# Scan units in pairs: the products of one tile shape of two units together

## The chip, the cores and the metric

The kernel runs on one core of a Trainium2 chip. The core has a matrix engine (TensorE, "PE" in the profile, with its weight loads as "PEld"), a vector engine (VectorE, "DVE"), a scalar engine (ScalarE, "ACT"), a general engine (GpSimd, "POOL") and a queue that issues DMA transfers (SyncE, "SP"). Each engine runs its own list of instructions in order, and they wait for each other through semaphores. TensorE writes into PSUM, which has eight banks of 512 float32 columns on 128 partitions. The metric is the time of one execution in microseconds (us), the median of several runs.

## The reference

Two stages. The first is a chunked scan (a state space layer) over 4 batches of 8 heads, 768 steps, head size 32, state size 16; the second is a gated feed-forward layer over the 3072 resulting rows of 256.

```
for each chunk of the sequence:
    M       = (C B^T) * exp(cum_i - cum_j) * causal
    y       = M x + (C state) * exp(cum)
    state   = decay_full * state + sum_j decay_from_j * B_j x_j
x    = y as rows of 256
gate = sigmoid(x @ w_gate);  val = x @ w_val
out  = (gate * val) @ w_out
```

All numbers are float32. The feed-forward matrices are 256 x 1536 (twice) and 1536 x 256.

## The kernel before, in words

The sequence is cut into 6 chunks of 128 steps. A **unit** is one chunk of one batch, with all 8 heads: 24 units, numbered u = 4 x chunk + batch. Behind each chunk, 512 rows go through the feed-forward layer: 12 pairs of a gate product and a value product, then 4 output products (one for each batch). From chunk 1 on these products run on operands that are split in a high and a low part of type fp32r, three passes for a gate or value product of 128 input rows and a 512- and a 256-column pass for an output product. The feed-forward work of chunk k is what TensorE does while the units of chunk k + 1 are computed in between.

A unit of chunk 1 or later has these steps on TensorE, and others around them:

- `products`: B and C are transposed (`pt`, L375 and L376, in a bank of the pool `ps_mm`), and ScalarE copies them to `bct` (L380, L384).
- `multiply`: B by C, four matmuls of 32 rows by 128 columns, one for each quarter of the partitions, which run side by side in the four tiles of that shape. Each writes 256 columns of one of four banks (`pcb`, L397). The pool `ps_cb` has one such tile, so the four banks hold one unit's products, half full.
- `decays`: VectorE's scan makes the matrix of decays (`ab`, L408). `before`: VectorE makes `cd` (L424), C times the decay from the chunk's start.
- `result`: VectorE multiplies `pcb` by the decays into `m` (L430). Then TensorE adds in one bank (`py`, pool `ps_y`, one bank) the part of the state (`py<-cd,sb`, L447, two matmuls of 128 x 128) and the part of the chunk (`py<-m,xn`, L453, eight matmuls of 128 rows by 32 columns, four side by side). In the same step follows the `multiply` of the next unit. So a unit's block on TensorE has three tile shapes: 128 x 128, 128 x 32, 32 x 128. A float32 matmul shows as two passes, the transposes as one.
- ScalarE takes `py` to the high part (L463), VectorE subtracts for the low part (L466) and transposes the rest (L471), from which `state` updates the state (L477) and the matrix `sb` (L485, mostly GpSimd).

Gate and value products (`pg`, `pv`, L699), output products (`po`, L728 for 512 columns and L729 for 256) and the transposes share the three banks of `ps_mm` in turn. A gate product is emptied by ScalarE's sigmoid (L654), a value product by VectorE's multiplication `g<-pv,g` (L669); then ScalarE rounds (L673) and GpSimd subtracts (L675) to make the two parts `h` that the output product needs. An output product is emptied by ScalarE's copy (L733) and VectorE's addition (L735), and its row block is written out (L741).

The order of all engines' instructions is written by a planner when the kernel is built (`run`): each task is a generator of steps with an engine, a cost, what it needs and makes, and a due time. The planner keeps a clock for each engine and picks, among the steps that can begin first, the task that is due first. The constants `UNIT_T`, `UNIT_D`, `AHEAD` and `STATE` set the due times of units, their loads and their state updates against the feed-forward work of the chunk; `FFN1` is where chunk 1's products are due. What the planner knows is costs and due times; the chip runs each engine's list in that order and waits where data is late.

## Time and profile before

| | before |
|---|---|
| median of 3 runs | 390.72 us (390.13 to 391.47) |
| profiled execution: its own time, its span | 389.6 us, 387.8 us |
| TensorE, weight loads busy | 378.4 us (98%), 287.4 us (74%) |
| VectorE, ScalarE, GpSimd busy | 197.0 us, 151.1 us, 159.7 us |
| output products of chunk 0, then chunk 1's gate products begin | 72.3 us, 102.4 us |
| gate products of chunks 2, 3, 4, 5 begin | 162.2, 220.7, 279.0, 334.2 us |

A row of the timeline has the start in the span, the time that the group takes, the engine, the line of the program, the operation, the tiles written and read, the shape, and the count of instructions merged. The ends of matmuls are modelled and overlap the next start, so TensorE's pace is read from start to start. A remark in brackets tells how long the engine had been idle and what it waited for.

### The profile page before, as it was taken

The page shows a single profiled execution, that of the slowest core. Times are in us where ns is not written, and L with a number is a line of the kernel's source. Part 1 is how long each engine was busy: PE and PEld are TensorE (multiplying, and loading weights), DVE is VectorE, ACT ScalarE, POOL GpSimd, SP SyncE. Part 2 cuts the span into 40 slices and gives each one's busy share as a digit, 9 for nine tenths or more (in the row PEclk, how much of TensorE's full clock was granted, in tenths as well). Part 3 has the DMA queues.
Part 4 walks back from the last instruction along what each step waited for, and adds up shares of the span by engine and source line. Part 5 has one row for each costly group of instructions (what it writes and reads, how often), then busy time and mean ns, then how long its engine had stood idle before and what let it go on. Part 6 is the DMA issues. An engine that isn't in the chain of part 4 may idle for free.

```text
span 387.8 us, 6198 instructions
## 1 busy us (share of the span) xinstructions
PE 378.4 (98%) x2368; PEld 287.4 (74%) x2368; DVE 197.0 (51%) x310; ACT 151.1 (39%) x319; POOL 159.7 (41%) x136
## 2 busy tenths in 40 slices
PE   8789999999999999999999999999999999999995
PEld 4444444677788778878788878788878788888884
DVE  3776878977746477856454356452323320122200
ACT  2564655434456521244441243440243430244400
POOL 2353354475899941035460054460033340045410
PEclk9758999999999999999999999999999999999999
DMA  7999782083700297333314513312100000000000
GB/s 86 236 368 385 100 217 77 5 165 103 124 13 1 24 214 167 56 93 87 45 44 103 94 38 88 40 50 49 47 2 0 2 0 29 27 0 2 0 27 29
DMA packets 107462, 31.39 MB, mean 81 GB/s; under 512 B 76554, under 2 KB 102730, under 8 KB 107434
## 3 DMA queue, kind: packets, MB, share of 16 engines
q1 hardware_dynamic: 107434, 31.01, 34.6%
q8 instruction: 19, 0.31, 0.3%
q14 instruction: 9, 0.07, 0.1%
HBM read 27.66 MB, written 3.34 MB: 80 GB/s over the span
## 4 chain that ended last, share of the span: by engine, by line
PE 92%; SPq 3%; DMA 2%; issue 1%; ACT 0%; POOL 0%; DVE 0%; ACTq 0%
PE pv L699 21%; PE pg L699 21%; PE po L728 15%; PE po L729 7%; PE pg L690 6%; PE po L721 6%; PE pv L690 5%; PE pcb L397 3%; PE py L453 3%; PE py L447 2%; DMA wr<-in_moe_w_val_dram 2%; SPq L267 1%; SPq L253 1%; SPq L293 1%; PE pt L375 1%
## 5 line engine op out<-in xcount | busy, mean ns | idle before, releaser
L675 POOL TENSOR_TENSOR h<-g,h 128x512 fp32r<-128x512 f32 x60 | 87.2, 1454 | 101.0 <-ACT h L673 100.9
L728 PE MATMUL po<-w,h 128*128 128x512 f32 x240 | 86.6, 403 | 0.0
L699 PE MATMUL pg<-xh,w 128*128 128x512 f32 x240 | 85.0, 395 | 0.0
L699 PE MATMUL pv<-xh,w 128*128 128x512 f32 x240 | 84.6, 393 | 0.0
L669 DVE TENSOR_TENSOR g<-pv,g 128x512 f32<-128x512 f32 x60 | 41.3, 688 | 83.7 <-PE pv L699 74.0
L673 ACT CAST h<-g 128x512 fp32r<-128x512 f32 x60 | 37.3, 621 | 80.3 <-DVE g L669 80.3
L729 PE MATMUL po<-w,h 128*128 128x256 f32 x240 | 67.4, 281 | 0.0
L728 PEld LDWEIGHTS po<-w,h 128*128 128x128 f32 x240 | 45.1, 188 | 12.9 <-issue 2.0
L699 PEld LDWEIGHTS pv<-xh,w 128*128 128x128 f32 x240 | 45.0, 188 | 11.4 <-issue 1.7
L654 ACT ACTIVATE g<-pg 128x512 f32<-128x512 f32 x72 | 43.0, 598 | 25.0 <-PE pg L690 15.2
L699 PEld LDWEIGHTS pg<-xh,w 128*128 128x128 f32 x240 | 45.0, 188 | 9.7 <-issue 0.3
L408 DVE TENSOR_TENSOR_SCAN ab<-ab,delta 128x1024 f32<-128x1024 f32 x20 | 47.5, 2378 | 4.1 <-DMA ab<-a_z 4.1
L699 PE MATMUL pg<-xl,w 128*128 128x512 f32 x120 | 46.8, 390 | 0.0
L699 PE MATMUL pv<-xl,w 128*128 128x512 f32 x120 | 46.7, 389 | 0.0
L729 PEld LDWEIGHTS po<-w,h 128*128 128x128 f32 x240 | 45.3, 189 | 0.2
L485 POOL TENSOR_TENSOR sb<-st,of_h 128x256 f32<-128x256 f32 x20 | 20.5, 1027 | 59.5 <-DVE st L477 48.3
L430 DVE TENSOR_TENSOR m<-pcb,ab 128x1024 f32<-128x1024 f32 x20 | 24.4, 1220 | 25.4 <-PE pcb L397 25.3
L323 POOL TENSOR_TENSOR wr<-wr 128x512 int32<-128x512 int32 x18 | 21.8, 1216 | 33.9 <-ACT wr L321 29.7
L733 ACT COPY o<-po 128x256 f32<-128x256 f32 x20 | 7.4, 372 | 62.5 <-PE po L729 60.7
L735 DVE TENSOR_TENSOR o<-po,o 128x256 f32<-128x256 f32 x20 | 8.5, 423 | 43.4 <-ACT o L733 43.2
L699 PEld LDWEIGHTS pv<-xl,w 128*128 128x128 f32 x120 | 22.5, 188 | 4.5
L699 PEld LDWEIGHTS pg<-xl,w 128*128 128x128 f32 x120 | 22.6, 188 | 4.3
(92 smaller groups left out, 428.1 us busy)
## 6 DMA issues: line engine op xcount, KB each, us to landing
ab<-a_z SPq DMA_DIRECT2D x20, 512.0 KB
wr<-in_moe_w_gate_dram SPq DMA_DIRECT2D x6, 512.0 KB
wr<-in_moe_w_val_dram SPq DMA_DIRECT2D x6, 512.0 KB
wr<-in_moe_w_out_dram SPq DMA_DIRECT2D x6, 512.0 KB
out_dram<-o SPq DMA_DIRECT2D x24, 128.0 KB
xn<-in_x_dram SPq DMA_DIRECT2D x10, 256.0 KB
bn<-in_B_dram SPq DMA_DIRECT2D x40, 32.0 KB
cn<-in_C_dram SPq DMA_DIRECT2D x40, 32.0 KB
```

Of the source, the lines that this page charges most:

```text
L323: nc.gpsimd.tensor_tensor(out=lw.bitcast(I32), in0=hw.bitcast(I32), in1=lw.bitcast(I32), op=ALU.add)
L408: nc.vector.tensor_tensor_scan(out=t.rearrange("p h l -> p (h l)"), data0=t.rearrange("p h l -> p (h l)"), data1=delta.rearrange("p h l -> ...
L430: nc.vector.tensor_tensor(out=self.second()[:, :, :L].rearrange("p (q g) l -> p q g l", g=NG), in0=self.pcb[:, :, : NG * L].rearrange("p q ...
L654: nc.scalar.activation(gs[k, f], pm, AF.Sigmoid)
L669: nc.vector.tensor_tensor(out=g, in0=pm, in1=g, op=ALU.mult)
L673: copies[eng](hh, g)
L675: engines[eng].tensor_tensor(out=hl, in0=g, in1=hh.bitcast(F32), op=ALU.subtract)
L690: nc.tensor.matmul(pm, whole[f // 2 * 2 + j][:, kt, fs], xb[0][0][:, kt], start=(kt == 0), stop=(kt == NK - 1))
L699: nc.tensor.matmul(pm, w[:, part, kt, fs], xx[:, kt], start=(i == 0), stop=(i == 3 * NK - 1))
L721: nc.tensor.matmul(acc[:, :DM], hs[k, f][:, js], whole[NF + f // 2][:, f % 2], start=(f == 0), stop=(f == NF - 1))
L728: nc.tensor.matmul(acc, hh, w.rearrange("p i m -> p (i m)"), start=(f == 0), stop=False, skip_group_check=True)
L729: nc.tensor.matmul(acc[:, :DM], hl, w[:, 0, :], start=False, stop=(f == NF - 1), skip_group_check=True)
```

## The change

From chunk 2 on, the two units of a pair of batches (0 and 1, 2 and 3) are one task (`results`). On TensorE first come both units' `py<-cd` matmuls (128 x 128), then both units' `py<-m` matmuls (128 x 32). The first unit's `py` is in `ps_y` as before, the second unit's takes one of the three banks of `ps_mm` until its results are taken; ScalarE and VectorE empty the second unit's first. `multiply` now makes a tile `pcb` of the same four banks for two units: each bank holds 256 columns of the one and 256 of the other. From chunk 2 on it is a task of its own (`multiply_after`, due as early as can be), which waits for the results of the two units before and both transposed copies. Units of chunk 1 stay single; the last of them is followed by the B by C products of the first two units of chunk 2.

Further, the due times change (all units of a chunk are due at one time, their loads 21.9 us ahead of it), steps of units are tied to their predecessor's in order (`bct`, `cd`), three steps of chunk 0 get a planned dependency on the transfers from the tiles that they overwrite (`held`), and the last output product of the last chunk is split: its twelve passes of 512 columns go to its bank, and the twelve low passes of 256 columns to a bank of their own behind them (`po`), with an addition of their own (L811 of the new program).

```diff
-FFN1 = 106.4
-UNIT_T = -15.3
-UNIT_D = 11.6
-AHEAD = 35.0
-STATE = 18.1
+FFN1 = 107.3
+UNIT_T = 3.4
+UNIT_D = 0.0
+AHEAD = 21.9
+STATE = 14.7
...
-            needs = [("bc", u), ("cb", u - 2), ("cd", u - 2)] + ([("x", 0, NB - 1)] if c == 1 else [])
+            needs = [("bc", u), ("bct", u - 1 if c > 1 else -1), ("cb", u - 2), ("cd", u - 2)] + ([("x", 0, NB - 1)] if c == 1 else [])
...
-            then = NB <= u < NB * NCH - 1
-            if then:
-                yield step("pe", 1.9, needs + [("bct", u + 1)], [("y", u), ("cb", u + 1)], cb=1)
-            else:
-                yield step("pe", 1.25, needs, [("y", u)])
+            then = [u + 1] if b < NB - 1 else [u + 1, u + 2]
+            yield step(
+                "pe", 1.25 + 0.65 * len(then), needs + [("bct", v) for v in then], [("y", u)] + [("cb", v) for v in then],
+                cb=1,
+            )
...
-            if then:
-                units[u + 1].multiply()
+            multiply(*(units[v] for v in then))
...
+    def multiply(*two):
+
+        pcb = ps_cb.tile([P, NQ, 2, NG * L], F32, tag="pcb", name=f"pcb{two[0].nm}")
+        for i, u in enumerate(two):
+            u.pcb = pcb[:, :, i]
+            for q in range(NQ):
+                qs = slice(32 * q, 32 * q + 32)
+                nc.tensor.matmul(
+                    pcb[:, q, i], u.bct[qs, 0], u.bct[qs, 2:4].rearrange("p g l -> p (g l)"), start=True, stop=True,
+                )
+
+    def multiply_after(*us):
+
+        then = [u + 2 for u in us]
+        yield step("pe", 1.3, [("y", u) for u in us] + [("bct", u) for u in then], [("cb", u) for u in then], cb=1)
+        multiply(*(units[u] for u in then))
+
+    def results(*two):
...
+        needs = [("lo", us[0] - 2), ("lo", 2 * NB - 1)] + [(k, u) for u in us for k in ("xn", "cd") + ("bdec",) * more] + [("S", u - NB) for u in us]
+        yield step("pe", 2.05, needs, [("y", u) for u in us], banks=1)
+        for t, pool, tag in zip(two, (ps_y, ps_mm), ("py", "mm")):
+            t.py = pool.tile([P, NG, LB], F32, tag=tag, name=f"py{t.nm}")
+
+        for t in two:
+            for g in range(NG):
+                nc.tensor.matmul(
+                    t.py[:, g, :L], sb[t.b][:, g].rearrange("p q d -> p (q d)"), t.cd,
+                    start=(g == 0), stop=False, skip_group_check=True,
+                )
+        for t in two:
+            xn = got["xn", c, t.b // 2][:, t.b % 2]
+            for g in range(NG):
+                for q in range(NQ):
+                    nc.tensor.matmul(
+                        t.py[32 * q : 32 * q + 32, g, : t.w], xn[:, NQ * g + q, :], t.m[:, NG * q + g, : t.w],
+                        start=False, stop=True, skip_group_check=True,
+                    )
+
+        for t, u in zip(two[::-1], us[::-1]):
...
+        last = (k, j) == (NCH - 1, NB - 1)
...
+            if last:
+                nc.tensor.matmul(acc, hh, w.rearrange("p i m -> p (i m)"), start=(f == 0), stop=(f == NF - 1))
+                continue
...
+            low = ps_mm.tile([P, 512], F32, tag="mm", name="po")
+            for f in range(NF):
+                nc.tensor.matmul(
+                    low[:, :DM], hs[k, f][:, 1, js], wo[f // 2][:, f % 2, 0, :], start=(f == 0), stop=(f == NF - 1)
+                )
...
+            if last:
+                yield step("dve", DVE_HALF)
+                nc.vector.tensor_tensor(out=o, in0=low[:, :DM], in1=o, op=ALU.add)
...
-        task(due, f"result{u.nm}", u.result())
+        if c < 2:
+            task(due, f"result{u.nm}", u.result())
+        elif b % 2:
+            if u.u < NB * NCH - 1:
+                task(-300.0, f"then{u.nm}", multiply_after(u.u - 1, u.u))
+            task(due, f"result{u.nm}", results(pair.pop(), u))
+        else:
+            pair.append(u)
```

What it does to the lists of instructions shows at three places. In the names, `pg3_3` is the gate product of chunk 3 and column block 3, `py4_1` the result of chunk 4, batch 1; the last number is the tile's own.

TensorE before, among the gate and value products of chunk 3, at unit 1 of chunk 4:

```order
L699 MATMUL pg3_3_2292<-xh3_1685,w2_733 128x512
L447 MATMUL py4_1_2307<-cd4_1_2188,sb1_115 128x128 x2
L453 MATMUL py4_1_2307<-m4_1_2094,xn4_0_1798 32x144 x8
L397 MATMUL pcb4_2_2318<-bct4_2_2299 128x256 x4
L699 MATMUL pv3_3_2328<-xh3_1685,w3_887 128x512
```

One unit's block: its two result shapes and, behind them, the B by C products of the next unit.

TensorE now, for units 0 and 1 of chunk 4:

```order
L760 MATMUL pv3_3_2274<-xh3_1787,w3_887 128x512
L519 MATMUL py4_0_2287<-cd4_0_2214,sb0_114 128x128 x2
L519 MATMUL py4_1_2288<-cd4_1_2252,sb1_115 128x128 x2
L527 MATMUL py4_0_2287<-m4_0_1966,xn4_0_1790 32x144 x8
L527 MATMUL py4_1_2288<-m4_1_1987,xn4_0_1790 32x144 x8
L375 MATMUL pt4_3_2313<-eye_88,bn4_1_1818 128x128
L376 MATMUL pt4_3_2313<-eye_88,cn4_1_1823 128x128
```

Both units' results stand in one block of two shapes; the transposes of unit 3 follow it in place of B by C products.

TensorE now, a gate product later, where the B by C products of units 2 and 3 stand:

```order
L760 MATMUL pg3_4_2316<-xl3_1788,w4_915 128x512
L760 MATMUL pg3_4_2316<-xh3_1787,w4_915 128x512
L489 MATMUL pcb4_2_2337<-bct4_2_2268 128x256 x4
L489 MATMUL pcb4_2_2337<-bct4_3_2328 128x256 x4
L760 MATMUL pv3_4_2365<-xh3_1787,w5_933 128x512
```

The B by C products of the two units stand together, by themselves, between a gate and a value product.

VectorE before, at the `cd` of unit 3 of chunk 4:

```order
L669 TENSOR_TENSOR g3_7_2428<-pv3_7_2421,g3_7_2428 128x512
L424 TENSOR_TENSOR cd4_3_2458<-bct4_3_2442,pp4_3_2247 128x128
L430 TENSOR_TENSOR m4_3_2362<-pcb4_3_2471,ab4_3_1958 128x8x128
L466 TENSOR_TENSOR xl4_2216<-py4_2_2460,xh4_2215 128x2x128
L669 TENSOR_TENSOR g3_8_2476<-pv3_8_2479,g3_8_2476 128x512
```

VectorE now, from the products of unit 2 with its decays to the same `cd`:

```order
L507 TENSOR_TENSOR m4_2_2346<-pcb4_2_2337,ab4_2_1875 128x8x128
L730 TENSOR_TENSOR g3_4_2351<-pv3_4_2365,g3_4_2351 128x512
L507 TENSOR_TENSOR m4_3_2349<-pcb4_2_2337,ab4_3_1880 128x8x128
L469 SCALAR_TENSOR_TENSOR st0_110<-st0_110,pp4_0_1862,tr4_0_2372 128x32
L730 TENSOR_TENSOR g3_5_2394<-pv3_5_2387,g3_5_2394 128x512
L401 SCALAR_TENSOR_TENSOR ab5_0_2281<-ab5_0_2281,delta_109 128x1024
L417 TENSOR_TENSOR cd4_3_2434<-bct4_3_2328,pp4_3_2407 128x128
```

The scan of the next chunk's first unit (L401) now stands directly ahead of this `cd`; before, a gate-value product stood there. Chunks 2, 3 and 4 have the second pair's subtraction (`xl`) directly behind another such scan.

More of the change, by code (lines that the diff above doesn't have):

```diff
@@ L392, in multiply @@
         def multiply(self):
-            self.pcb = ps_cb.tile([P, NQ, 512], F32, tag="pcb", name=f"pcb{self.nm}")
-            for q in range(NQ):
-                qs = slice(32 * q, 32 * q + 32)
-                nc.tensor.matmul(
-                    self.pcb[:, q, : NG * L], self.bct[qs, 0],
-                    self.bct[qs, 2:4].rearrange("p g l -> p (g l)"), start=True, stop=True,
-                )
+            multiply(self)
         def decays(self):
@@ L660, in value @@
         if k == 0:
-            yield step("dve", DVE_MM, [("sig", k, f)], [("h", k, f)], banks=-1, g=-1)
+            held = {8: [("p",)], 9: [("a_p",)], 10: [("a_z",)]}.get(f, [])
+            yield step("dve", DVE_MM, [("sig", k, f)] + held, [("h", k, f)], banks=-1, g=-1)
         else:
@@ L714, in proj @@
                 yield step(
-                    "pe", PROJ_T / 3 if k else 1.8, needs,
+                    "pe", 0.92 if last else PROJ_T / 3 if k else 1.8, needs,
                     [("proj", k)] if j == NB - 1 and f + 4 == NF else [], banks=int(f == 0),
@@ L803, in initial @@
     def initial():
-        keys = ("y", "cb", "cd", "lo", "t", "w", "tp", "scan", "bdec", "mult", "S", "pu", "tu", "ph", "early", "tr0")
+        keys = ("y", "bct", "cb", "cd", "lo", "t", "w", "tp", "scan", "bdec", "mult", "S", "pu", "tu", "ph", "early", "tr0")
         made = [(k, u) for k in keys for u in range(-6, 0)]
@@ L829, in tile_ssd_then_gated_ffn @@
         task(-50.0 + i, name, gen)
+    pair = []
     def unit(due, c, b):
```

32 lines of the change are left out of this document (30 added, 2 removed).

## The prediction

> **What bounds the kernel now.** I read the page's busy times and its chain of waits first, then the busy time by stage, then TensorE's instructions in order of time.
>
> ```profile
> PE 378.4 (98%) x2368; PEld 287.4 (74%) x2368; DVE 197.0 (51%) x310; ACT 151.1 (39%) x319; POOL 159.7 (41%) x136
> PE 92%; SPq 3%; DMA 2%; issue 1%; ACT 0%; POOL 0%; DVE 0%; ACTq 0%
> 162.20:220.50 58.30, 58.30 (x363) 47.48 (x361) 30.47 (x45) 20.44 (x43) 20.39 (x16) 1.00 0.34 72
> 279.00:334.20 55.20, 55.20 (x321) 45.36 (x320) 13.95 (x23) 18.78 (x37) 15.42 (x12) 1.00 0.02 8
> ```
>
> TensorE is the chain that ends last: 92% of it, and in the stage from 162.2 to 220.5 us (gate, value and output products of chunk 2, with the units of chunk 3) it is busy for all of 58.30 us, VectorE for 30.47 and GpSimd for 20.39, at granted clock 1.00. So a microsecond taken from TensorE's own queue there is a microsecond of the result, as long as the work around it stays hidden. The question is whether a busy TensorE is computing. The instructions around one unit say no:
>
> ```profile
> 229.91 0.39 PE L699 MATMUL pg<-xl,w 128*128 128x512 f32 x1
> 230.13 0.40 PE L699 MATMUL pg<-xh,w 128*128 128x512 f32 x1
> 230.37 0.61 PE L447 MATMUL py<-cd,sb 128*128 128x128 f32 x4
> 230.90 0.70 PE L453 MATMUL py<-m,xn 128*32 128x144 f32 x16
> 231.53 0.71 PE L397 MATMUL pcb<-bct 32*128 32x256 f32 x8
> 232.18 0.50 PE L699 MATMUL pv<-xh,w 128*128 128x512 f32 x1
> 232.51 0.39 PE L699 MATMUL pv<-xl,w 128*128 128x512 f32 x1
> 232.74 0.40 PE L699 MATMUL pv<-xh,w 128*128 128x512 f32 x1
> ```
>
> Times here are from start to start, since matmuls overlap. The numbers after the line (128\*128, 128\*32, 32\*128) are the tile shape. From 230.37 to 232.18 the unit takes 1.81 us, and the product behind it needs 0.33 us to its successor instead of the 0.23 of the next row: 0.10 more. One unit costs 1.91 us. Against that, the pace at which passes of one shape follow each other:
>
> ```profile
> 31.39 1.72 PE pv L690 x4
> 200.78 0.27 PE L375 MATMUL pt<-eye,bn 128*128 128x128 f32 x1
> 200.89 0.27 PE L376 MATMUL pt<-eye,cn 128*128 128x128 f32 x1
> ```
>
> Four 512-column fp32 passes take 1.72 us, 0.43 each, so 144 columns are 0.121 and 256 are 0.215; two 128-column passes start 0.11 apart. The unit has four passes on 128\*128 (0.44), sixteen on 128\*32, which run four abreast, so four rounds (0.48), and eight on 32\*128, two rounds (0.43): 1.35 us. The other **0.56 us is spent on changing tile shape three times**. Two more places price the pieces:
>
> ```profile
> 309.03 0.60 PE L447 MATMUL py<-cd,sb 128*128 128x128 f32 x4
> 309.57 0.64 PE L453 MATMUL py<-m,xn 128*32 128x128 f32 x16
> 310.14 0.50 PE L699 MATMUL pv<-xh,w 128*128 128x512 f32 x1
> 310.48 0.39 PE L699 MATMUL pv<-xl,w 128*128 128x512 f32 x1
> 66.01 1.88 PE L690 MATMUL pv<-xh,wr 128*128 128x512 f32 x4
> 67.82 0.71 PE L397 MATMUL pcb<-bct 32*128 32x256 f32 x8
> 68.46 0.33 PE L375 MATMUL pt<-eye,bn 128*128 128x128 f32 x1
> 68.63 0.27 PE L376 MATMUL pt<-eye,cn 128*128 128x128 f32 x1
> ```
>
> The last unit has no B by C product behind it: 1.11 us plus 0.11 in its successor, 1.22, against 0.44 + 4 x 0.108 = 0.87 at pace: **0.35 for two shapes and back**. A B by C product by itself: the passes before it should end at 66.01 + 1.72 = 67.73, it starts at 67.82 (0.09 late), takes 0.64 against 0.43, and the transpose behind it 0.17 against 0.11: **0.36**, or 0.40 where a 512-column product comes behind it and loses 0.10 instead of 0.06.
>
> The Trainium skill, TensorEngine Tiling (Array Packing), section Tiling Modes, says that changing the tiling mode, not just the tile, drains TensorE. The gap of 0.09 us ahead of 67.82 is of that kind; the page names no second cost, and here the larger part is a weight load that nothing covers (0.10 in the product behind). By the drain alone, an estimate, 18 changes fewer at 0.09 would save 1.6 us in place of the 3.46 below and, with the other terms as they are, end at 389.4; the sum goes by the rows.
>
> **The change part by part.** *Shape changes.* Before, chunks 2 to 5 hold 15 units with three shapes and one with two: 15 x 0.56 + 0.35 = 8.75 us of switching. In the new order stand eight pairs. One (chunk 2, units 0 and 1) keeps its B by C product behind it: 0.56. Seven have only two shapes: 7 x 0.35 = 2.45. The B by C products of six pairs stand by themselves, three ahead of a transpose and three ahead of a value product: 3 x 0.36 + 3 x 0.40 = 2.28. The pair for chunk 2's start rides behind a unit of chunk 1 as one did before. Together 5.29: **3.46 us less**. The passes are the same in number, columns and type.
>
> *Rounds of a pair.* No trace row shows four B by C rounds in a row. Lower bound of their cost: the pace, 0.215 each, since the four rounds of 128\*32 follow at pace; upper bound: each second unit pays the uncovered load again, 0.10, plus about 0.03 in its 128\*32 rounds, 8 x 0.13 = 1.0 us. Below the pace is excluded, the columns must stream. I take the pace, because the 128\*32 rounds are the nearest row; the 1.0 stays for the range.
>
> *The end.* The last output product is split: its low part goes to a bank of its own, behind the rest.
>
> ```profile
> 383.28 0.40 PE L728 MATMUL po<-w,h 128*128 128x512 f32 x1
> 383.52 0.28 PE L729 MATMUL po<-w,h 128*128 128x256 f32 x1
> 383.84 0.37 ACT L733 COPY o<-po 128x256 f32<-128x256 f32 x1 [1.05 <-PE po L729]
> 384.24 0.42 DVE L735 TENSOR_TENSOR o<-po,o 128x256 f32<-128x256 f32 x1 [0.99 <-ACT o L733]
> ```
>
> ScalarE's copy and VectorE's first addition now lie under twelve low passes (12 x 0.11 = 1.3 us against 0.37 + 0.42); behind the last pass comes only the new addition, as long as the one at 384.24. The copy and its hand-over go: 384.24 - 383.84 = **0.40 us less**. Twelve 512-column passes in a row may also gain some hundredths; counted as nothing.
>
> *Waits added.* A B by C product of a pair waits for both units' transposed copies, and the value product is queued behind it on TensorE.
>
> ```profile
> 201.19 0.37 ACT L380 COPY bct<-pt 128x256 f32<-128x256 f32 x1
> 201.46 0.63 ACT L384 ACTIVATE bct<-pt,of_g 128x128 f32<-128x128 f32 x2
> ```
>
> The copies end at 202.09, 1.20 us behind the transpose at 200.89. Between the second unit's transposes and its rounds stand a value product (six passes at 0.23, 1.38 us) and the first unit's two rounds (0.43): 1.81 us of cover, 0.6 spare. Cost nothing; without the cover up to 1.2 us at each of six places.
>
> The second wait is tighter. In chunks 3 and 4, VectorE's queue now holds, behind the B by C product of units 2 and 3: two products with the decays, two gate-value products, an update of the state, a scan, and then the fourth unit's `cd`, which TensorE's next pair needs (the `cd` of one unit stands at 187.15 before, right behind a gate-value product).
>
> ```profile
> 174.01 1.23 DVE L430 TENSOR_TENSOR m<-pcb,ab 128x1024 f32<-128x1024 f32 x1 [0.37 <-PE pcb L397]
> 181.09 0.69 DVE L669 TENSOR_TENSOR g<-pv,g 128x512 f32<-128x512 f32 x1 [2.03 <-PE pv L699]
> 181.70 2.28 DVE L408 TENSOR_TENSOR_SCAN ab<-ab,delta 128x1024 f32<-128x1024 f32 x1
> 187.15 0.28 DVE L424 TENSOR_TENSOR cd<-bct,pp 128x128 f32<-128x128 f32 x1
> 179.80 1.29 POOL L675 TENSOR_TENSOR h<-g,h 128x512 fp32r<-128x512 f32 x1 [1.01 <-ACT h L673]
> 182.52 2.55 POOL L675 TENSOR_TENSOR h<-g,h 128x512 fp32r<-128x512 f32 x1 [1.43 <-ACT h L673]
> ```
>
> TensorE's cover is six gate and value products and the first unit's four passes: 6 x 1.38 + 0.44 = 8.7 us. VectorE's work ahead of the second gate-value product (2 x 1.23 + 0.69 and an update) is over under 4 us, but that product can't begin before its value product ends, 3 x 1.38 = 4.1; then 0.69 + 2.28 + 0.28 = 3.25, so 7.4. But GpSimd's `h` took 2.55 us instead of 1.29 where it met the scan that began at 181.70: the two take turns. One `h` in front of the `cd` makes 8.7, no slack; two make it 1.3 us late. Two such places: 0 to 2.6 us. I charge **0.7**, nearer to no second turn, because the waiting `h` usually is one.
>
> *Loads.* The units' loads are due later against their chunk, and several swap places on SP's queue.
>
> ```profile
> 205.59 0.37 SPq L272 DMA_DIRECT2D ab<-a_z  x1
> 209.91 2.29 DVE L408 TENSOR_TENSOR_SCAN ab<-ab,delta 128x1024 f32<-128x1024 f32 x1 [3.01 <-DMA ab<-a_z]
> ```
>
> A load of decays lands 4.3 us after its issue, and here VectorE already waited 3.01 us for one while TensorE was busy throughout. Cost nothing while VectorE has 28 of 58 us free; a load late by more than that wait would join the second wait above.
>
> Sum: 3.46 + 0.40 - 0.7 = **3.2 us less**. The profiled execution took 389.6 us (span 387.8), so 386.4 for one like it; it lies 1.1 under the median of 390.72. From the median: **387.5 us**.
>
> **The rivals.** *VectorE and GpSimd take one turn more* at both places of the fourth `cd`: 2.6 instead of 0.7, so 389.4. For it: the sum has no slack. Against: it needs two `h` in a row. The Trainium skill, GPSIMD Engine Reference, section Specifications, says that GpSimd's SBUF interfaces are shared with VectorE and contended by instructions with two SBUF inputs; the scan and `cd` have two, and the row of 2.55 us agrees.
>
> *The third bank (slower).* A pair's second `py` sits in one of the three banks through which gate, value and output products rotate. It is freed by a copy, a subtraction and a transpose, some 1.0 us (0.37, 0.41 and 0.21 below), and TensorE can run a gate and a value product, 2.76 us, on the other two. In the second pair of chunks 2, 3 and 4 a scan stands directly ahead of the subtraction.
>
> ```profile
> 175.15 0.41 DVE L466 TENSOR_TENSOR xl<-py,xh 128x256 fp32r<-128x256 f32 x1
> 176.24 0.21 DVE L471 STREAM_TRANSPOSE tr<-py 128x32 f32<-128x32 f32 x1
> L463 ACT CAST xh<-py 128x256 fp32r<-128x256 f32 x20 | 7.4, 371 | 23.8 <-PE py L453 23.8
> ```
>
> With the whole scan and one `h` in the way it is held 1.0 + 2.28 + 1.29 = 4.6 us, TensorE stands 1.8, at three places 5.4, so 392.9. It decides from 1.5 us per place (4.4 in all). Against: a scan that began before the pair's products is partly over by then. The Trainium skill, TensorEngine Tiling (Array Packing), section Performance Considerations, warns that tiling doesn't speed the emptying of PSUM and that the copy may become the bottleneck; no row before shows it, TensorE never waits there.
>
> *The pair isn't one block:* the second unit's rounds pay their loads again, 1.0 us, 388.5.
>
> **How the numbers follow.** Forecast 0.66 (386.9 with no stall to 388.3), one turn more 0.16, pair not one block 0.09, third bank 0.09. About 0.3%, 1.17 us, can be told from no change here: faster is under 389.55, slower over 391.9. Faster: the forecast, the third rival and half of the first, 0.66 + 0.09 + 0.08 = 0.83. Same: the first's other half and a third of the bank rival, 0.11. Slower 0.06. Range 386.6 to 389.9: below 386.9 nothing is left to save but what rows rounded to 0.01 us hide in twenty sums (0.3), above it takes in two turns at both places with half a microsecond more.
>
> **What would show it.** Right: in the stages from chunk 1's products on, pairs of 0.9 us on 128\*128 and 1.0 on 128\*32, B by C products of four rounds in 1.07 us from start to start; TensorE still busy for the whole of each stage; the last DMA issue one VectorE addition after the last matmul. Wrong: a second unit's first round 0.3 us behind the first's last; TensorE waiting for `cd` or, at a gate product behind a pair, for a bank; scans late by their loads. The forecast falls if such waits sum to over 2 us.

## The result and the profile after

The changed kernel takes **387.64 us** (median of 7 runs, 387.16 to 389.84) against 390.69 us (7 runs, 389.42 to 391.47) for the kernel before on the same chip: a ratio of 0.9933, 95% interval 0.9916 to 0.9951. The forecast was 387.5 us, so it came out as forecast. In a later session it took 387.78 us (9 runs) against 390.44 us, ratio 0.9951 (0.9921 to 0.9982); one of the nine, at 943.83 us, was a disturbed execution that the ratio leaves out, the others lie between 386.19 and 391.98 us. One execution of it was profiled: 387.17 us, span 384.7 us.

First two lines of the changed kernel's page (busy times, chain of waits), then its busy time in the window of chunk 2's feed-forward work that was shown of before (length, then busy time and count for TensorE, its weight loads, VectorE, ScalarE, GpSimd, then granted clock, DMA share, GB/s):

```profile
PE 375.2 (98%) x2368; PEld 287.8 (75%) x2368; DVE 203.0 (53%) x311; ACT 149.8 (39%) x319; POOL 166.6 (43%) x136
PE 93%; SPq 3%; DMA 1%; DVE 1%; issue 1%; POOL 0%; ACT 0%
162.20:220.50 58.30, 58.30 (x365) 47.97 (x364) 31.49 (x45) 20.50 (x45) 23.21 (x16) 1.00 0.34 68
```

As many TensorE instructions as before, 3.2 us less of TensorE's time, and TensorE still busy for the whole window: two more of its instructions fall into the same 58.30 us. GpSimd was busy 6.9 us longer than before with the same work, 5 us of it in the sixty `h` (92.1 us, 1537 ns each on the average, against 87.2 us and 1454 ns before): they meet VectorE more often now.

The time splits at two events that both kernels have. The first low pass of chunk 1's first gate product is at 102.44 us before and at 103.46 us after:

```profile
102.44 0.39 PE L699 MATMUL pg<-xl,w 128*128 128x512 f32 x1
```

```profile
103.46 0.40 PE L760 MATMUL pg<-xl,w 128*128 128x512 f32 x1
```

From there to the start of the last matmul (383.52 us before, 381.23 us after, the twelfth of the row at 379.93 below) it is 281.09 us before and 277.77 us after: **3.32 us less**. Of this, 0.42 us is not saved but moved: two B by C rounds, those of chunk 2's second unit, now stand in the block of chunk 1's last unit, ahead of this stretch (the B by C products there take 1.07 us where they took 0.65), and before they stood in it. So TensorE's own queue lost 2.90 us. The tail gives some more. Before, the last matmul started at 383.52 us and the last write was issued at 384.70 us, 1.18 us later. After, 0.77 us (381.23 to 382.00): **0.41 us less**.

The last rows of TensorE, ScalarE and VectorE in the changed kernel:

```profile
379.93 1.58 PE L801 MATMUL po<-w,h 128*128 128x256 f32 x12
380.13 0.37 ACT L806 COPY o<-po 128x256 f32<-128x256 f32 x1 [0.55 <-PE po L790]
381.55 0.42 DVE L811 TENSOR_TENSOR o<-po,o 128x256 f32<-128x256 f32 x1 [0.59 <-PE po L801]
```

ScalarE's copy starts 0.2 us after the twelve low passes have begun; behind the last of them stands one VectorE addition.

A first pair of chunk 3 and its B by C products, as TensorE ran them:

```profile
171.77 1.05 PE L519 MATMUL py<-cd,sb 128*128 128x128 f32 x8
172.75 1.19 PE L527 MATMUL py<-m,xn 128*32 128x144 f32 x32
173.87 0.33 PE L375 MATMUL pt<-eye,bn 128*128 128x128 f32 x1
174.03 0.27 PE L376 MATMUL pt<-eye,cn 128*128 128x128 f32 x1
...
175.63 1.15 PE L489 MATMUL pcb<-bct 32*128 32x256 f32 x16
176.70 0.50 PE L760 MATMUL pv<-xh,w 128*128 128x512 f32 x1
177.04 0.40 PE L760 MATMUL pv<-xl,w 128*128 128x512 f32 x1
```

From start to start: 0.98 us for eight passes on 128\*128 and 1.12 us for eight rounds on 128\*32, 2.10 us, with 0.05 us more in the first transpose (0.16 against 0.11). At pace this work is 8 x 0.11 + 8 x 0.121 = 1.85 us, so switching is 0.30 us for this pair (0.31 without rounding), 0.25 inside the block and 0.05 behind it. Where a gate, value or output product follows a pair in place of a transpose, that product loses 0.10 to 0.11, and the switching is 0.36. The four B by C rounds take 1.07 us from 175.63 to 176.70.

TensorE waits for something new at the second pair of the same chunk, in chunk 4 likewise, and at one gate product. First the pair's rows on TensorE, then on VectorE, SP's queue and GpSimd:

```profile
185.04 1.14 PE L519 MATMUL py<-cd,sb 128*128 128x128 f32 x8
186.11 1.19 PE L527 MATMUL py<-m,xn 128*32 128x144 f32 x32
```

```profile
180.22 1.03 DVE L469 SCALAR_TENSOR_TENSOR st<-st,pp,tr 128x32 f32<-128x32 f32 x1
181.84 2.28 DVE L401 TENSOR_TENSOR_SCAN ab<-ab,delta 128x1024 f32<-128x1024 f32 x1
185.01 0.34 DVE L417 TENSOR_TENSOR cd<-bct,pp 128x128 f32<-128x128 f32 x1 [0.89 <-DMA pp<-a_p]
```

```profile
175.59 3.54 SPq L259 DMA_DIRECT2D bn<-in_B_dram  x4
179.23 2.10 SPq L259 DMA_DIRECT2D cn<-in_C_dram  x4
181.43 1.85 SPq L278 DMA_DIRECT2D pp<-a_p  x2
```

```profile
179.91 1.30 POOL L736 TENSOR_TENSOR h<-g,h 128x512 fp32r<-128x512 f32 x1 [2.95 <-ACT h L734]
182.65 2.55 POOL L736 TENSOR_TENSOR h<-g,h 128x512 fp32r<-128x512 f32 x1 [0.69 <-ACT h L734]
```

The first shape takes 1.07 us here instead of 0.98, so 0.09 us is lost; in chunk 4 the same block takes 1.13 us. VectorE had finished the scan at 184.12 us and stood idle 0.89 us, until the load of `pp` had landed. That load is the second of the row at 181.43 and was issued at 182.12 us. What held it was its place in SP's queue: behind eight loads of B and C, issued one after the other from 175.59 to 181.33, and another `pp`. Its buffer was free before, with the state update of 180.22 us, which ended at 181.25 (it took 1.03 us instead of 0.24 beside GpSimd's `h`). In the kernel before, this `pp` is loaded ahead of those eight.

The gate product is in chunk 4, at 251.94 us: TensorE's weight loads stood idle for 0.30 us ahead of it, until a `g<-pv,g` of 251.20 us had emptied a bank, and the product and its predecessor together take 0.15 us longer than such products do. That `g<-pv,g` is queued behind a scan (247.87 us) and a state update that took 0.99 us beside an `h`. The three places together cost 0.39 us (0.09, 0.15 and 0.15).

### The profile page after: what moved, and what is told of

It reads as the page before. It is cut to its first block, busy times and chain, and to the rows that moved or that the text cites. A ratio compares the mean times of both kernels' runs of the same rounds, so it can differ in the third digit from the quotient of the medians.

```text
span 384.7 us, 6190 instructions
## 1 busy us (share of the span) xinstructions
PE 375.2 (98%) x2368; PEld 287.8 (75%) x2368; DVE 203.0 (53%) x311; ACT 149.8 (39%) x319; POOL 166.6 (43%) x136
## 4 chain that ended last, share of the span: by engine, by line
PE 93%; SPq 3%; DMA 1%; DVE 1%; issue 1%; POOL 0%; ACT 0%
PE pv L760 22%; PE pg L760 21%; PE po L793 14%; PE po L794 7%; PE pg L751 6%; PE po L783 6%; PE pv L751 5%; PE pcb L489 3%; PE py L527 2%; PE py L519 2%; SPq L253 1%; SPq L267 1%; DMA wr<-in_moe_w_val_dram 1%; PE pt L375 1%; PE po L790 1%; PE py L446 1%
## 5 line engine op out<-in xcount | busy, mean ns | idle before, releaser
L736 POOL TENSOR_TENSOR h<-g,h 128x512 fp32r<-128x512 f32 x60 | 92.1, 1537 | 129.7 <-ACT h L734 129.6
L793 PE MATMUL po<-w,h 128*128 128x512 f32 x228 | 81.0, 399 | 0.0
L794 PE MATMUL po<-w,h 128*128 128x256 f32 x228 | 64.0, 281 | 0.0
L793 PEld LDWEIGHTS po<-w,h 128*128 128x128 f32 x228 | 42.8, 188 | 10.8 <-issue 0.2
L401 DVE TENSOR_TENSOR_SCAN ab<-ab,delta 128x1024 f32<-128x1024 f32 x20 | 49.2, 2461 | 2.5 <-DMA ab<-a_z 2.5
L794 PEld LDWEIGHTS po<-w,h 128*128 128x128 f32 x228 | 43.1, 189 | 0.3
L336 POOL TENSOR_TENSOR w<-wr,w 128x512 fp32r<-128x512 f32 x18 | 27.6, 1532 | 4.5 <-ACT w L334 4.4
L477 POOL TENSOR_TENSOR sb<-st,of_h 128x256 f32<-128x256 f32 x20 | 18.7, 940 | 20.9 <-DVE st L469 17.5
```

Of the source, the lines that this page charges most:

```text
L336: engines[eng].tensor_tensor(out=lo, in0=lw, in1=hi.bitcast(F32), op=ALU.subtract)
L401: nc.vector.tensor_tensor_scan(out=t.rearrange("p h l -> p (h l)"), data0=t.rearrange("p h l -> p (h l)"), data1=delta.rearrange("p h l -> ...
L736: engines[eng].tensor_tensor(out=hl, in0=g, in1=hh.bitcast(F32), op=ALU.subtract)
L793: nc.tensor.matmul(acc, hh, w.rearrange("p i m -> p (i m)"), start=(f == 0), stop=False, skip_group_check=True)
L794: nc.tensor.matmul(acc[:, :DM], hl, w[:, 0, :], start=False, stop=(f == NF - 1), skip_group_check=True)
```

## The experiments

Each is told as the ratio of its time to the kernel before on the same chip, and by one length that doesn't contain the run-to-run scatter of the start (last section): from the first low gate pass of chunk 1 to the last matmul, 281.09 us before, 277.77 us in the changed kernel. "The stretch" below is this length. It is that of one profiled execution of each kernel; where waits for loads lie in it, no run shows how much it varies.

### Unit by unit inside the block

```diff
         for t in two:
+            xn = got["xn", c, t.b // 2][:, t.b % 2]
             for g in range(NG):
                 nc.tensor.matmul(t.py[:, g, :L], ... t.cd, ...)
-        for t in two:
-            xn = got["xn", c, t.b // 2][:, t.b % 2]
             for g in range(NG):
                 for q in range(NQ):
                     nc.tensor.matmul(... xn ..., t.m ...)
```

Everything else is as in the changed kernel; in a pair's block the shapes now come 128\*128, 128\*32, 128\*128, 128\*32.

> The changed kernel, but inside a pair's block TensorE takes unit by unit: the first unit's 128 x 128 and 128 x 32 matmuls, then the second unit's. Tasks, due times, banks and the order around the block stay as changed; each of the eight pairs has two more changes of tile shape. Theory (the gain is shape changes saved): each pair pays 0.35 us again (the price of the two-shape block), 8 x 0.35 = 2.8, so 387.6 + 2.8 = 390.4 us, and the block of a pair lasts 2.45 us from its first start to the first start behind it, where the changed kernel has 2.10. Rival (the gain is the new order and due times, whatever stands inside a block): 387.6 us, within 0.5.

389.90 us (389.20 to 390.59), ratio 0.9983 (0.997 to 0.9996). The stretch is 280.13 us, 2.36 us longer than in the changed kernel. The same place on TensorE:

```profile
172.56 0.60 PE L520 MATMUL py<-cd,sb 128*128 128x128 f32 x4
173.09 0.70 PE L526 MATMUL py<-m,xn 128*32 128x144 f32 x16
173.72 0.71 PE L520 MATMUL py<-cd,sb 128*128 128x128 f32 x4
174.36 0.70 PE L526 MATMUL py<-m,xn 128*32 128x144 f32 x16
174.99 0.33 PE L375 MATMUL pt<-eye,bn 128*128 128x128 f32 x1
```

2.43 us from 172.56 to 174.99 against 2.10: the second `py<-cd` takes 0.64 us from start to start where the first takes 0.53, and each `py<-m` 0.63 where half of the joint one is 0.56. So a pair pays 0.33 us more, close to the 0.35 charged, and all eight 2.66. The stretch grew by less, because the waits at the second pairs and at the gate product (0.39 us) aren't there in this order. With nothing but the order of matmuls inside a block changed, 2.36 of the 3.3 us are gone: **the gain is the order of shapes**.

### The new due times with single units

Edit: the kernel before with the five new constants (`FFN1`, `UNIT_T`, `UNIT_D`, `AHEAD`, `STATE`) and nothing else.

> The kernel before with the five changed due constants alone (FFN1, UNIT_T, UNIT_D, AHEAD, STATE), units single. Theory (shape changes): the number of changes is that of before, so no gain: 390.7 us, or up to 1.5 more, because the last unit of a chunk now stands at the end of the output products and the next chunk's gate products wait for its result. Rival (the due times gave the gain): 387.9 us, the changed kernel without its 0.4 at the end.

394.04 us (393.63 to 394.57), ratio 1.0089 (1.0071 to 1.0108); the stretch is 284.69 us, 3.6 us longer than before. The waits of TensorE, summed by line and releaser (total us, times, longest), and the first of them:

```profile
PE pg L699 <- DVE xl L466: 3.0, 3, 1.0
162.46 0.50 PE L699 MATMUL pg<-xl,w 128*128 128x512 f32 x1 [1.01 <-DVE xl L466]
```

The last unit of a chunk now stands so close to the next chunk's gate products that these wait for its low part, at three places. The direction was as expected, the size larger. So the due times alone give no gain; with single units they cost 3.6 us. Pairs with the old due times were not run.

### The end alone

Edit: the kernel before with the split of the last output product and nothing else.

> The kernel before with the split of the last output product alone. Theory: from the start of the last matmul to the last issue of a write 0.78 us where before has 1.18, so 0.40 less: 390.3 us, which the times can hardly tell from before but the trace can. Rival (the copy's place on the path is taken by something else, as the wait for the bank): still 1.1 to 1.2 us.

390.20 us (389.15 to 392.32), ratio 0.9983 (0.9965 to 1.0001): by the time alone not to be told from no change. By the trace it does what the step said: last matmul at 386.42 us, last write issued at 387.19 us, 0.77 us, where it was 1.18. The stretch is 281.04 us, as before.

### A longer queue ahead of the fourth `cd`

```diff
             yield step("dve", 0.42, [("bct", u), ("pp", u), ...], [("cd", u)], port=True)
+            if b == 3 and c in (3, 4):
+                for i in range(4):
+                    nc.vector.tensor_tensor(out=spare_sb, in0=delta[..., :256], in1=delta[..., 256:512], op=ALU.mult)
```

Four multiplications of 256 columns whose results nobody uses stand ahead of the fourth unit's `cd` in chunks 3 and 4 (indexing shortened here).

> The changed kernel with four more VectorE multiplications of 256 columns (results unused, about 0.33 us each, 1.2 us together) directly ahead of the fourth unit's cd in chunks 3 and 4. The changed kernel's trace shows the second pair's first shape lasting 1.07 us instead of 0.98 at 185.04 us: 0.09 us of waiting. Theory (the cover of 8.7 us is used up, so any delay of that cd is paid in full): that shape lasts about 2.2 us at both places, 2.2 to 2.5 us more in all, 390.0 us. Rival (the 0.09 is no wait for cd, and slack remains): under 0.6 more in all, 388.0 us or less. If later gate products lose a bank too, more than 3 us.

390.40 us (389.09 to 392.85), ratio 1.0004 (0.9981 to 1.0026); the stretch is 281.20 us, 3.43 us longer than in the changed kernel. TensorE at the second pair of chunk 3, and VectorE's four:

```profile
183.90 0.60 PE L526 MATMUL py<-cd,sb 128*128 128x128 f32 x4
186.07 0.68 PE L526 MATMUL py<-cd,sb 128*128 128x128 f32 x4 [1.57 <-DVE cd L424]
186.68 1.19 PE L534 MATMUL py<-m,xn 128*32 128x144 f32 x32
182.89 2.83 DVE L419 TENSOR_TENSOR spare_sb<-delta 128x256 f32<-128x256 f32 x4
```

The first shape takes 2.78 us instead of 0.98: 1.8 us at this place, as much in chunk 4. The four were to take 1.2 us; they took 2.83, the first 1.45 beside GpSimd's `h` (which ended at 184.06), the others 0.43 each. Of these, 0.89 us are the time that VectorE stands idle at this place in the changed kernel (above); the other 1.9 us reach TensorE. So behind that idle time there is no slack, as the prediction said: a late `cd` is paid in full.

### The changed kernel again

No edit; it runs beside the next three on one chip.

> The changed kernel itself once more, beside the next three on one chip, so that these can be set against it and not only against the kernel before. Expected 387.6 us (387 to 388.3), first gate pass of chunk 1 to last matmul 277.8 us again.

387.78 us (9 runs), ratio 0.9951 (0.9921 to 0.9982): the time is the expected one. The stretch of this run isn't known; the comparisons below use that of the first.

### B by C behind the first pair

```diff
+FUSE = (0,)
...
+        then = [u + 2 for u in us] if two[0].b in FUSE and us[1] < NB * NCH - 1 else []
+        needs += [("bct", v) for v in then]
...
+        if then:
+            multiply(*(units[v] for v in then))
```

The B by C products of the third and fourth unit follow the first pair's `py<-m` directly; their own task is left out.

> The B by C products of the third and fourth unit of a chunk stand in the TensorE block of the first pair, directly behind its masked products, in place of a block of their own among the gate and value products. Theory (every change of tile shape costs about 0.2 us, whoever stands beside it): a block of three shapes changes three times (0.56 us in the kernel before), a two-shape block and a lone product five times (0.30 and 0.42 in the changed kernel), so 0.16 us less at three places, 0.5 us less in all: 387.1 us, first gate pass to last matmul 277.3. Rival (what counts is that products wait for their operands, and pairing only spaced them out): the products come nearer to their inputs, so the copies to bct are late, and the time is the changed kernel's or worse, 388 to 389 us.

388.01 us (385.53 to 391.75), ratio 0.9945 (0.9923 to 0.9966), no different from the changed kernel. The stretch of the profiled execution is 279.50 us, 1.7 us longer; that execution took 390.54 us, more than all but one of the twelve, so its waits may be longer than the usual. Three shape changes fewer (40 against 43 from 60 us on), but four waits, together 1.94 us; the largest on TensorE, and what VectorE did:

```profile
249.42 0.60 PE L523 MATMUL py<-cd,sb 128*128 128x128 f32 x4
250.91 0.71 PE L523 MATMUL py<-cd,sb 128*128 128x128 f32 x4 [0.89 <-DVE g L736]
249.58 0.68 DVE L418 TENSOR_TENSOR cd<-bct,pp 128x128 f32<-128x128 f32 x1 [1.70 <-DMA pp<-a_p]
```

And a first pair with the B by C products behind it:

```profile
175.41 1.05 PE L523 MATMUL py<-cd,sb 128*128 128x128 f32 x8
...
178.58 0.50 PE L766 MATMUL pv<-xh,w 128*128 128x512 f32 x1
178.92 0.40 PE L766 MATMUL pv<-xl,w 128*128 128x512 f32 x1
```

VectorE waits 1.70 us for the load of `pp`, and the fourth `cd` is 1.05 us late. The price of a change was as expected: this block and its successor lose 0.58 us (3.17 us from 175.41 to 178.58, of them 0.47 over the pace, and 0.11 behind it), the pair and the lone block of the changed kernel 0.31 and 0.42, so 0.15 us less at each of three places. Taking the waits off the stretch doesn't show it, since each wait also leaves the product behind it about 0.1 us longer and the changed kernel has waits of its own. So the theory held for the shapes, and the rival for the time; but what TensorE waited for was the load of `pp` and VectorE's queue, and no B by C product waited for a copy to `bct`.

### B by C behind every pair

Edit: `FUSE = (0, 2)`, and the loads, transposes and copies of the first two units of chunks 3, 4 and 5 due 45 us earlier.

> Also the B by C products of the next chunk's first pair stand behind the second pair's masked products; so that these pairs don't all fall to the end of the chunk, loads and transposes of the first two units of chunks 3 and 4 are due 45 us earlier. Theory: no B by C block stands alone any more, six fewer than in the changed kernel, 0.16 us each: 1.0 us less, 386.6 us, first gate pass to last matmul 276.8. Rival: the earlier loads and scans crowd VectorE and GpSimd, and a gate product or a pair waits once or more for 1.3 us, as in the run with new due times alone: 388 us or more.

390.04 us (388.64 to 394.50), ratio 1.0014 (0.9981 to 1.0046). The rival was right about the waits and the time. 37 shape changes instead of 43, and the stretch is 280.25 us: waits of 0.28, 0.77, 1.58 and 1.02 us, together 3.65. Without them it would be 276.6 or a little less. The largest:

```profile
181.48 0.53 PE L767 MATMUL pv<-xh,w 128*128 128x512 f32 x1 [1.34 <-DVE g L737]
179.66 1.16 DVE L419 TENSOR_TENSOR cd<-bct,pp 128x128 f32<-128x128 f32 x1 [2.08 <-DMA pp<-a_p]
```

The value product waits for a bank that `g<-pv,g` empties; that instruction is queued on VectorE behind a `cd` that waited 2.08 us for its load of `pp`.

### Four buffers for `pp`

```diff
-        t = ld.tile([P, L], F32, tag="pp", name=f"pp{c}_{b}")
+        t = ld.tile([P, L], F32, tag="pp", name=f"pp{c}_{b}", bufs=NBUF + 1)
...
-            "p": load(1, 0.3, [("cd", u - NBUF), ("pu", u - NBUF), ("a_p",)], ...),
+            "p": load(1, 0.3, [("cd", old), ("pu", old), ("a_p",)], ...),
```

`old` is `u - NBUF - 1`: the load waits for one unit earlier. The changed kernel otherwise.

> The load of p gets a fourth buffer, so that it no longer waits until the state update of three units earlier has read its own; the planner then also puts the second pair somewhat earlier. Theory (the fourth cd was 0.1 us late because its load of p was, and the load because the buffer came free late): the first shape of the second pair takes 0.98 us in chunks 3 and 4 instead of 1.07, so 0.2 us less or the same time within what can be told, 387.4 to 387.7 us. Rival (VectorE's queue with its turns with GpSimd makes it late): still 1.07 or more.

386.75 us (385.63 to 388.09), ratio 0.9908 (0.9877 to 0.994); the stretch is 277.48 us, 0.29 us shorter than in the changed kernel. The second pair of chunk 3, and the fourth `cd` on VectorE:

```profile
180.27 1.05 PE L519 MATMUL py<-cd,sb 128*128 128x128 f32 x8
181.25 1.19 PE L527 MATMUL py<-m,xn 128*32 128x144 f32 x32
174.56 0.28 DVE L417 TENSOR_TENSOR cd<-bct,pp 128x128 f32<-128x128 f32 x1
```

0.98 us from 180.27 to 181.25, and the fourth `cd` is made right behind the third (of 174.06), 5.7 us ahead of its pair. In this kernel the load of its `pp` stands ahead of those of B and C in SP's queue, and the wait is gone: it was the load's. The pair stands about 5 us earlier than in the changed kernel, so this isn't the old order with a faster load. Against the changed kernel's 387.78 us the intervals overlap, so a gain over it isn't shown by the time.

### Both: every pair, four buffers

Edit: the two edits above together, with the first two units of chunks 3, 4 and 5 due 30 us earlier.

> The run with all B by C blocks behind a pair, with four buffers for p as well, and the first two units of chunks 3 and 4 due 30 us earlier instead of 45. Theory now: what made the run without the fourth buffer no faster than the kernel before were waits of the value product (0.77, 1.58, 1.02 us) behind VectorE's wait for the load of p; the two B by C changes that it removed saved 0.09 us at each of six places. Without those waits, first gate pass to last matmul 276.9 us against 277.8 in the changed kernel and 277.5 with four buffers alone, and 386.3 us. Rival (the other loads that come earlier, those of the scan's input, make VectorE wait as long): waits of 0.5 us or more stay, and the time is 387.5 us or more.

390.00 us (388.76 to 391.83), ratio 0.9996 (0.9976 to 1.0016). The theory missed: the waits for `pp` are gone, and two others stand elsewhere, 1.84 and 1.5 us. Its 0.09 us for a place was too low as well (0.15, above). The stretch is 279.97 us.

```profile
146.51 0.39 PE L801 MATMUL po<-w,h 128*128 128x256 f32 x1 [1.68 <-POOL h L743]
143.45 3.00 POOL L743 TENSOR_TENSOR h<-g,h 128x512 fp32r<-128x512 f32 x1 [0.20 <-ACT h L741]
171.34 0.33 PE L377 MATMUL pt<-eye,bn 128*128 128x128 f32 x1 [1.34 <-DVE g L737]
168.41 2.29 DVE L403 TENSOR_TENSOR_SCAN ab<-ab,delta 128x1024 f32<-128x1024 f32 x1 [1.90 <-DMA ab<-a_z]
```

At 144 us an output product waits for GpSimd's last `h`, which took 3.00 us beside a scan; at 170 us a transpose waits for a bank behind a scan that had waited 1.90 us for its own load. The rival named this second load.

### Both: first pair, four buffers

Edit: `FUSE = (0,)` and four buffers for `pp`.

> The run with the B by C products of the third and fourth unit behind the first pair, with four buffers for p as well. Theory: the waits of 0.3, 0.3 and 1.05 us that stood in that run go with the load of p; three changes of 0.09 us fewer than in the changed kernel remain: first gate pass to last matmul 277.2 us, 386.5 us. Rival (the pair stands too near to its own scans): a wait of about 1 us stays at the second pair, 387.5 us.

387.17 us (385.98 to 388.03), ratio 0.9908 (0.9883 to 0.9932); the stretch is 278.44 us. The waits for `pp` are gone, but two of 0.57 and 0.71 us stand at a gate product of chunks 3 and 4:

```profile
180.78 0.50 PE L766 MATMUL pg<-xh,w 128*128 128x512 f32 x1 [0.41 <-DVE g L736]
175.05 2.29 DVE L402 TENSOR_TENSOR_SCAN ab<-ab,delta 128x1024 f32<-128x1024 f32 x1 [2.88 <-DMA ab<-a_z]
```

Behind the scan that waited 2.88 us for its load, VectorE empties its queue without a pause, and `g<-pv,g` comes at 180.04 us, late for the bank. Without the two waits, and the 0.11 us that each leaves in the product behind it, the stretch would be 276.94 us, 0.54 below the kernel with four buffers alone: 0.18 a place (0.15 by the rows of the blocks alone) and not the 0.09 of the expectation.

### First unit's results first

```diff
-        for t, u in zip(two[::-1], us[::-1]):
+        for t, u in zip(two, us):
...
-            if t.b == 1:
+            if t.b == 0:
```

In the changed kernel the second unit's results are emptied first, because they hold one of the three rotating banks. Here the first unit's are.

> The changed kernel with the results of a pair emptied first unit first, so that the bank that the second unit's values took from the gate products comes free about 1 us later. Theory (the banks that are left suffice): no wait of TensorE above 0.3 us appears, first gate pass to last matmul 277.8 us as before, 387.6 us. Rival (the third bank decides): the gate products behind a pair wait 0.5 to 1 us at each of six pairs, 3 us or more, 390.5 us or more.

386.84 us (385.65 to 387.95), ratio 0.9902 (0.9873 to 0.9931). No gate product waits longer than in the changed kernel (the weight loads stand idle for 0.26 us ahead of one in chunk 4, where it was 0.30); the stretch is 277.57 us, 0.2 us shorter. With the other order of the state updates the planner puts the load of the fourth unit's `pp` one place earlier in SP's queue, first behind the eight of B and C, and the wait at the second pair is gone:

```profile
184.36 0.30 DVE L417 TENSOR_TENSOR cd<-bct,pp 128x128 f32<-128x128 f32 x1 [0.98 <-DMA pp<-a_p]
185.67 1.05 PE L519 MATMUL py<-cd,sb 128*128 128x128 f32 x8
```

The `cd` ends a microsecond ahead of the pair. It still waited 0.98 us for its load, which was issued at 182.08 us though its buffer had been free since 176.80: the place in SP's queue decides, not the buffer. The third bank decides nothing here.

Of the kernels tried, three have a median below the changed kernel's 387.78 us (386.75 in the same session, 386.84 and 387.17 in a later one) and beat the kernel before; against the changed kernel their intervals overlap, so none is shown to beat it.

## Why the prediction was right

- **Bound.** TensorE's order of shapes was to set the time. Shown: with the same instructions in the other order inside the block (unit by unit), 2.36 us of the gain are gone; with the due times alone the kernel gets slower.
- **Shape changes.** 3.46 us were charged, at 0.7 of waits: a net 2.76 us on TensorE. Measured: 2.90 net. Added up block by block from start to start, at the paces of the prediction, the switching is 8.73 us before (8.75 in the sum) and 5.31 us in the changed kernel without its waits (5.29): 3.42 us saved. The single prices moved by hundredths: 0.31 for the three pairs with a transpose behind them, 0.36 for the others where 0.35 was taken, 0.42 and 0.43 for a lone B by C block ahead of a value product where 0.40 was. So the shapes came out as worked out, and the net is near by a bit of luck: the waits are 0.39 us and not 0.7, and 0.13 us more, which no single row holds, are lost outside the blocks. That a drain of 0.09 us per change is not the whole price is shown: 18 changes fewer at 0.09 us would be 1.6 us. The Trainium skill, TensorEngine Tiling (Array Packing), section Tiling Modes, names the drain only; by it 389.4 us was worked out, and the measured 387.64 us speaks against it as the whole of the cost.
- **Rounds of a pair.** Taken at the pace, with up to 1.0 us more held open. Measured: 1.07 us for four B by C rounds, first change included, as stated. A pair's two shapes took 0.98 and 1.12 us where the sign of being right had 0.9 and 1.0, which is the pace alone; the switching inside the block is the difference. The rival that the pair isn't one block falls.
- **The end.** 0.40 us charged, 0.41 measured, and 0.41 again with the split alone.
- **Waits added, second unit's copies.** Cost nothing charged; no such wait in the trace.
- **Waits added, fourth `cd`.** Here the step failed in its mechanism, and its 0.7 us was too much: the two places cost 0.09 and 0.15 us. It was reasoned that VectorE's queue had no slack against 8.7 us of cover because GpSimd's `h` stretches the scan, and 0.7 us was charged. The rows show VectorE idle for 0.89 us ahead of this `cd`, scan and turns done, waiting for `pp`, whose load stood behind eight others in SP's queue. GpSimd's turn also stretched the state update that frees the load's buffer (1.03 against 0.24 us), but that ended 0.9 us before the load was issued. Moving the load ahead in the queue, as four buffers do, takes the wait away. That a late `cd` is paid in full was right (1.8 us at each of two places with the longer queue).
- **Loads.** That several loads swap places on SP's queue was seen; "Cost nothing while VectorE has 28 of 58 us free" was the wrong test. So the wait that was charged to turns with GpSimd belongs here, and the condition that the prediction added, that a load later by more would join the second wait, is what happened. Free time on the average doesn't help where the engine's queue is in order: one load late by 1 to 2 us holds a `cd`, then the `g<-pv,g` behind it, then a bank, then TensorE. In the changed kernel that costs 0.24 us at the two pairs; in the variants with tighter blocks it cost up to 3.65 us, more than these saved.
- **The rivals.** One more turn: both `h` meet VectorE (the first stretches the state update, the second takes 2.55 us), but not on the chain. The third bank: one wait of 0.15 us at a gate product in the changed kernel, for a value product's bank on VectorE's queue behind a scan, and none longer with the pair's bank held longer; the rival needed 1.5 us at each of three places. The Trainium skill, TensorEngine Tiling (Array Packing), section Performance Considerations, warns that emptying PSUM may become the limit; in the changed kernel only that 0.15 us is of this kind, and in the variants the waits for a bank came from a load, not from the copies.

## What to carry to other kernels

Where TensorE is busy throughout, read its rows from start to start against the pace of its columns: each change of tile shape showed as about 0.1 us at the change and 0.05 to 0.1 us in the product behind it, and doing the same products of two units together paid that once. Before moving such blocks closer together, follow each operand back to its load, to the buffer that the load waits for, and to what stands ahead of it in the queue that issues it: the tighter orders here saved 0.5 to 1 us of changes and lost 1.3 to 3.7 us to loads and to the in-order queues. And due times belong to the order they were tuned for: alone they made this kernel 3.6 us slower.

## What the runs showed of the hardware

The first low gate pass of chunk 1 came at 102.3 to 105.4 us in the profiles, 3 us apart behind nearly the same work, and executions of one kernel scatter by 2 to 3 us. Most of the difference between profiles lies in one interval; that the scatter of one kernel has this cause too is inferred, since one execution of each was profiled. TensorE's granted clock is 0.50 from 20 to 30 us in every profile, and somewhere after 30 us it rises to 1.00. The same window of three profiles (columns as above; the end alone, the changed kernel, the longer queue):

```profile
30.00:40.00 10.00, 10.00 (x18) 4.30 (x19) 5.79 (x11) 4.78 (x9) 3.78 (x4) 0.75 1.05 384
```

```profile
30.00:40.00 10.00, 10.00 (x22) 4.31 (x22) 5.17 (x10) 4.61 (x9) 2.32 (x3) 0.89 1.06 362
```

```profile
30.00:40.00 10.00, 10.00 (x24) 4.52 (x23) 5.35 (x11) 5.18 (x9) 3.12 (x4) 0.99 1.04 359
```

With a clock of 0.75, 0.89 and 0.99 there, chunk 1's first low gate pass came at 105.39, 103.46 and 102.31 us: the later the clock opens, the later everything behind it. From that pass on, two kernels with the same order and no waits agree to a few hundredths of a microsecond (281.09 and 281.04 us), which is why the stretch tells variants apart that the medians don't. The Trainium skill, TensorE: Matmul & The Clock Gate, Part 1, has the full clock granted after some 3.4 us of sustained matmuls, 0.5 us more or less. Here TensorE was busy 8.6 of the 10 us from 20 to 30 us in the changed kernel and the clock stayed at 0.50; no run here shows what delays it.

Turns with GpSimd also stretch VectorE's instructions, not only GpSimd's: of four multiplications of 256 columns the first took 1.45 us beside an `h` and the other three 0.43 each behind its end, and the state update took 1.03 us where it takes 0.24 alone. A long scan that had begun before the `h` kept its time (2.28 us), and the `h` beside it paid (2.55 us); a scan that began while an `h` ran took longer itself (3.28 us at 252.78 us in the changed kernel, where the next `h` also took 3.28).
